# Moving the token counts behind the third unit of the first expert, and h splits and a conversion behind the last gates

## The chip, the core and the metric

The kernel runs on one core of one Trainium2 chip, as one program. The metric is the device time in microseconds (us). TensorE (PE) multiplies matrices, and its weight loads (PEld) overlap them; VectorE (DVE), ScalarE (ACT) and GpSimd (POOL) work element by element; SyncE (SP) issues most of the DMA transfers. Each engine works through its own list of instructions and waits on semaphores for the others.

## The reference

Three stages in a row, all in float32, on 2304 tokens (4 batches of 576) with 512 features.

```
phi(x) = exp(h - max h) / sqrt(m),  h = x @ omega.T - |x|^2/2         # random features, q and k
num = phi(q) @ (phi(k).T @ v);  den = phi(q) @ sum(phi(k)) + 1e-6;  x = num / den

logits = normalized(x) @ normalized(expert_emb).T / tau                # routing over 8 experts
expert_idx = argmax(logits);  gate_w = softmax(logits)[expert_idx]
out[mask] = gate_w * (relu(x[mask] @ w1[e]) @ w2[e])                   # for each expert e that has tokens

silu(x @ w_gate) * (x @ w_val) @ w_out                                 # d_ff = 1536; these weights are doubles
```

## The kernel before

A float32 operand is used as two parts (`hi_lo`): ScalarE casts it to the high part (L92), VectorE subtracts to get the low part (L93). A product is then three TensorE products, high with high, high with low, low with high (`HALVES`). Both parts of an operand have to be there before all three can run, but the first two need the high part of the stationary weights alone.

**The first stage** (L420 to L690) goes over 18 tiles of k and 18 of q, 128 tokens each. It writes x transposed into a large tile (`xp`) and collects logits for the routing, in two groups of nine tiles (`Routing`, two batches each). The second group's routing is not finished when the stage ends. What is left of it is `rest`, a generator: softmax, one-hot choice and gates on VectorE (`softmax`, `gates`), then `counts`. `counts` multiplies the one-hot sums `oc` by a matrix of ones (L327), transposes the gates `gt` (L333) and stores them to memory (L336), and finds for each batch the expert that most of its tokens chose (`dom_i`) and how many tokens chose others (`ext_i`, and their total `tot_i`).

**The second stage** runs one expert for each of the four batches, that batch's dominant one, on all 576 tokens. An expert has four units of `mm1` (each 256 columns of the hidden layer, two blocks of 24 products, L884) and then four of `mm2` (48 products each, L903). Each unit fetches its weights (512 KB, L384) into two raw buffers and splits them into `wp` tiles. ReLU (L890, high part) and its low part (L891) follow each block. A table `todo` (from L1035) says what else is written at the end of which unit: `(0, 1): routing_end` means at batch 0, after the second unit. `routing_end` runs `rest` to its end and lets the engines load `tot_i` into a register (L1008), by which they branch past a loop for tokens of other experts. In that loop nothing runs where the total is zero. The weight splits of the third unit are held in program order.

**The third stage** computes both gated products (12 slices of the hidden layer, named f, by three groups of tokens, named g) with seven products instead of eight (L1120), in the PSUM tiles `a`, `b` and `c`. `tokens` writes after each product what ScalarE, VectorE and GpSimd do with it: copies, sums (L1085), silu (L1088), and the last product (L1091, L1092), which goes to memory as `hds` (L1093). Beside it the doubles are turned into float32 by integer work (`words`: one step on ScalarE, L782, five on VectorE, L784 to L802).

**The fourth stage** is the output product (L1191). For f from 0 to 11 it loads h (`hidden`, 128 by 1024, L1183), splits it, and adds three products for each of eight token tiles into eight PSUM tiles `o_ps`, which take the banks that the third stage held. Output weights `wos` are converted two at a time, by `out_ahead`, and split by `out_weights`.

The order of each engine's list is made by a scheduler with a model of the engines' times; only some instructions are held in the order in which the program is written (`keep_in_program_order`), or behind one that is named (`issue_after`). In the stretch of the counts, ScalarE's copy L335, its load L1008 and the third unit's weight cast L92 follow one another.

Of the kernel before, what the change touches and what calls it, by code (L numbers as in the profile page):

```python
# [14 lines left out]
AF = mybir.ActivationFunctionType  # L15
ALU = mybir.AluOpType
# [12 lines left out]
def attention_moe_ffn_kernel(  # L29
# [815 lines left out]
    with ExitStack() as p2:  # L845
# [184 lines left out]
        def split_begin():  # L1030
# [2 lines left out]
            tc.keep_in_program_order(nc.scalar.activation(out=silu_set, in_=zero, func=AF.Silu))  # L1033

        todo = {  # L1035
            (0, 1): routing_end, (0, NU - 1): no_y,
            (0, NU + NC - 2): near_extras, (0, NU + NC - 1): extras,
            (2, 0): lambda: weights_ahead(0), (2, NU - 1): lambda: list(split_y(0)),
            (3, 0): lambda: weights_ahead(1), (3, NU - 1): lambda: list(split_y(1)),
# [27 lines left out]
    with ExitStack() as p3:  # L1067
# [7 lines left out]
        def tokens(f, g):  # L1075
# [9 lines left out]
                nc.vector.tensor_tensor(out=out, in0=bank_of[k], in1=out, op=ALU.add)  # L1085

            def silu(x):
                nc.scalar.activation(out=x, in_=x, func=AF.Silu)  # L1088

            def last_product():  # L1090
                nc.vector.tensor_tensor(out=cc[:, 0], in0=bank_of["a"], in1=cc[:, 0], op=ALU.mult)  # L1091
                nc.gpsimd.tensor_tensor(out=cc[:, 1], in0=c22, in1=cc[:, 1], op=ALU.mult)  # L1092
                nc.sync.dma_start(  # L1093
                    out=hds[f][:, g * GW:(g + 1) * GW], in_=cc.rearrange("p a n -> p (a n)")
                )
# [80 lines left out]
    with ExitStack() as p4:  # L1176
        op = p4.enter_context(tc.tile_pool(name="op", bufs=6, reuse_waits="tile"))
        ops = p4.enter_context(tc.tile_pool(name="ops", bufs=8, space=PSUM, reuse_waits="tile"))

        def hidden(f, t0, n, slot, width):  # L1180
            raw = wpool.tile([128, 2, NC * FU], F32, tag="wp", name="h32")
            raw = raw.rearrange("p a n -> p (a n)")[:, 0:n * 128]
            nc.sync.dma_start(out=raw, in_=hds[f][:, t0 * 128:(t0 + n) * 128])  # L1183
            at = slot * 2 * width
            h = arena[:, at:at + 2 * n * 128].rearrange("p (a n) -> p a n", a=2)
            hi_lo(h[:, 0], h[:, 1], raw)
            return h

        def product(p, h, f, i):
            for k, (x, a) in enumerate(HALVES):  # L1190
                nc.tensor.matmul(  # L1191
                    p, h[:, x, i * 128:(i + 1) * 128], wos[f][:, a],
                    start=(f == 0 and k == 0), stop=(f == NF - 1 and k == 2),
                )

        def store(p, t):
            o = op.tile([128, DM], F32, tag="o", name="o")
            nc.scalar.copy(o, p)  # L1198
            nc.sync.dma_start(out=out[t * 128:(t + 1) * 128, :], in_=o)

        n_h = 0
        for t0 in range(0, NTI, 8):
            n = min(8, NTI - t0)
            ps = [ops.tile([128, DM], F32, tag="o", name="o_ps") for _ in range(n)]
            if n == 8:
                for f in range(NF):
                    if t0 == 0:
                        if f not in wos:
                            out_weights(f)
                        if f == 1:  # L1210
                            out_ahead(6)
                        elif f in (4, 6):
                            out_ahead(f + 4)
                    h = hidden(f, t0, n, n_h % 3, 1024)
                    n_h += 1
                    for i in range(n):
                        product(ps[i], h, f, i)
                        if f == NF - 1:
                            store(ps[i], t0 + i)
            else:  # L1220
                hs = [hidden(f, t0, n, f, 256) for f in range(NF)]
                for i in range(n):
                    for f in range(NF):
                        product(ps[i], hs[f], f, i)
                    store(ps[i], t0 + i)
# [67 lines left out]
```

## Time and profile before

| | us |
|---|---|
| median of 3 runs | 789.08 (787.39 to 791.02) |
| the profiled execution | 789.36 |
| its span, first to last instruction | 787.3 |
| TensorE matmuls busy | 762.6 (97%) |
| VectorE busy | 506.3 (64%) |
| ScalarE busy | 361.8 (46%) |
| GpSimd busy | 153.4 (19%) |
| mean granted clock of TensorE | 0.988 |

The span is the time that the profile shows; the execution's own time lies 2.1 us above it. TensorE is nearly always busy, so a busy share of another engine says little: what counts is which instruction TensorE waits for. [...]

### The profile page before, as it was taken

To read this page: it belongs to the slowest core of one execution; us is meant where nothing else is said; L and a number is where in the kernel's file an instruction comes from. 1 tells how busy PE (TensorE), PEld (TensorE's weight loads), DVE (VectorE), ACT (ScalarE), POOL (GpSimd) and SP (SyncE) were. 2 spreads that over 40 slices of the span, in tenths; PEclk is the share of its full clock that TensorE was granted. 3 is DMA by queue.
4 is the path that set the end of the run, shared out by engine and by line. 5 is a ranking of instruction groups with operands and counts; after the bars stand their busy time and mean duration, and the time that the engine had idled before them with its cause. 6 is when DMAs were issued, how large, how long until landed. Compare 5 with 4: busy or idle time off the path is not lost.

```text
span 787.3 us, 14727 instructions
## 1 busy us (share of the span) xinstructions
PE 762.6 (97%) x5860; PEld 713.7 (91%) x5861; DVE 506.3 (64%) x878; ACT 361.8 (46%) x789; POOL 153.4 (19%) x201
## 2 busy tenths in 40 slices
PE   9999899959999999999999999999999999999997
PEld 8877777859999999999999999999999988888886
DVE  5788999554243478585887776898887777212220
ACT  5888668553132243343554444444454633241231
POOL 3864344200001404104111111111211110000000
PEclk9999989979999999999999999999999999999999
DMA  8744642122233323420132232233323555353233
GB/s 276 218 143 160 201 147 99 42 83 83 82 98 134 96 82 134 97 107 1 41 114 94 94 134 94 95 134 124 122 111 112 172 169 158 113 210 107 81 98 116
DMA packets 33908, 94.02 MB, mean 119 GB/s; under 512 B 4240, under 2 KB 8352, under 8 KB 33832
## 3 DMA queue, kind: packets, MB, share of 16 engines
q1 hardware_dynamic: 33672, 92.99, 35.3%
q8 instruction: 47, 0.77, 0.4%
q14 instruction: 29, 0.24, 0.1%
q10 hardware_dynamic: 160, 0.02, 0.0%
HBM read 74.05 MB, written 18.95 MB: 118 GB/s over the span
## 4 chain that ended last, share of the span: by engine, by line
PE 70%; DVE 1%; DMA 1%; issue 1%; ACT 0%; ACTq 0%; DVEq 0%
PE o_ps L1191 19%; PE a L1120 18%; PE b L1120 9%; PE two L884 7%; PE two L903 5%; PE third L903 5%; PE c L1120 5%; PE third L884 2%; DMA h<-hds 1%; DVE xp L93 0%; DVE cc L1085 0%; DVE cv_t L798 0%; ACT xp L92 0%; DVE raw L795 0%; ACT o L1198 0%
## 5 line engine op out<-in xcount | busy, mean ns | idle before, releaser
L1191 PE MATMUL o_ps<-xp 128*128 128x512 f32 x648 | 147.5, 389 | 0.7 <-DVE cc L1091 0.4
L1191 PEld LDWEIGHTS o_ps<-xp 128*128 128x128 f32 x648 | 121.5, 188 | 26.6 <-DVE cc L1091 0.8
L504 ACT ACTIVATE ph<-two,bias 128x128 f32<-128x128 f32 x288 | 78.1, 387 | 29.4 <-DVE bias L495 23.1
L93 DVE TENSOR_TENSOR xp<-h,xp 128x1024 fp32r<-128x1024 f32 (+1 forms) x36 | 34.4, 958 | 82.3 <-ACT xp L92 81.8
L884 PE MATMUL two<-xp,wp 128*128 128x288 f32 x576 | 82.0, 301 | 4.5 <-ACT wp L92 2.5
L884 PEld LDWEIGHTS two<-xp,wp 128*128 128x128 f32 x576 | 79.5, 193 | 5.3 <-ACT wp L92 2.8
L1092 POOL TENSOR_TENSOR cc<-c,cc 128x384 f32<-128x384 f32 x36 | 39.8, 1110 | 225.0 <-ACT cc L1088 191.9
L930 POOL TENSOR_TENSOR y_g<-y_g,t 128x192 f32<-128x192 f32 (+3 forms) x29 | 37.3, 1306 | 181.5 <-DVE t L915 181.5
L92 ACT CAST xp<-h 128x1024 fp32r<-128x1024 f32 (+1 forms) x36 | 30.0, 838 | 79.1 <-PE o_ps L1191 62.0
L92 ACT CAST wp<-raw 128x1024 fp32r<-128x1024 f32 x32 | 33.6, 1049 | 58.4 <-PE two L903 29.5
L1088 ACT ACTIVATE cc<-cc 128x384 f32<-128x384 f32 x72 | 37.3, 525 | 49.7 <-DVE cc L1085 49.5
L903 PE MATMUL third<-h_all,wp 128*128 128x288 f32 x384 | 52.8, 296 | 0.0
L903 PE MATMUL two<-h_all,wp 128*128 128x288 f32 x384 | 52.2, 296 | 0.0
L903 PEld LDWEIGHTS third<-h_all,wp 128*128 128x128 f32 x384 | 51.7, 189 | 0.0
L903 PEld LDWEIGHTS two<-h_all,wp 128*128 128x128 f32 x384 | 51.5, 189 | 0.0
L487 DVE TENSOR_REDUCE mx<-two 128x8 f32<-128x1024 f32 x36 | 43.9, 1220 | 8.3 <-PE two L477 8.1
L93 DVE TENSOR_TENSOR wp<-raw,wp 128x1024 fp32r<-128x1024 f32 x30 | 39.9, 1329 | 11.0 <-ACT wp L92 10.7
L1120 PE MATMUL a<-xp,over_y 128*128 128x384 f32 x216 | 43.3, 335 | 0.0
L1120 PEld LDWEIGHTS a<-xp,over_y 128*128 128x128 f32 x216 | 38.3, 188 | 0.0
L1120 PE MATMUL a<-xp,wh 128*128 128x384 f32 x144 | 37.0, 338 | 0.0
L891 DVE SCALAR_TENSOR_TENSOR h_all<-two,h_all 128x576 fp32r<-128x576 f32 x24 | 18.1, 756 | 26.2 <-ACT h_all L890 26.2
L890 ACT ACTIVATE h_all<-two 128x576 fp32r<-128x576 f32 x24 | 15.5, 652 | 38.7 <-PE two L884 38.7
(211 smaller groups left out, 1529.5 us busy)
## 6 DMA issues: line engine op xcount, KB each, us to landing
raw<-in_w_dram SPq DMA_DIRECT2D x68, 512.0 KB, 3.7
hds<-cc SPq DMA_DIRECT2D x36, 384.0 KB, 2.3
h<-hds SPq DMA_DIRECT2D x24, 512.0 KB, 3.5
q<-in_qx_dram SPq DMA_DIRECT2D x18, 512.0 KB, 3.6
k<-in_kx_dram SPq DMA_DIRECT2D x14, 512.0 KB, 4.5
v<-in_vx_dram SPq DMA_DIRECT2D x18, 276.0 KB, 4.2
out_dram<-o SPq DMA_DIRECT2D x18, 256.0 KB, 2.6
h<-hds SPq DMA_DIRECT2D x12, 128.0 KB, 2.2
```

What stands on the lines that cost most here:

```text
L92: go = nc.scalar.copy(hi, src)
L93: low = lo_eng.tensor_tensor(out=lo, in0=src, in1=hi.bitcast(F32), op=ALU.subtract)
L487: nc.vector.tensor_reduce(out=mx.rearrange("p (c a) -> p a c", a=2), in_=p.rearrange("p a (h m) -> p a h m", m=M), axis=AX.X, op=ALU.max,)
L504: nc.scalar.activation(out=ph[:, h, :], in_=p[:, h % 2, h // 2 * M:(h // 2 + 1) * M], func=AF.Exp, bias=bias[:, h:h + 1],)
L884: nc.tensor.matmul(ps[:, j], w[:, a, c, f * 128:(f + 1) * 128], xv[:, c, b, j * HB:(j + 1) * HB], start=(c == 0 and n == 0), stop=(c == NC ...
L891: nc.vector.scalar_tensor_tensor(out=h2[:, 1], in0=ps, scalar=0.0, in1=h2[:, 0].bitcast(F32), op0=ALU.max, op1=ALU.subtract,)
L903: late["mark"][ENG.PE] = nc.tensor.matmul(ps[:, j], w[:, a, f, :], h[:, b, j * HB:(j + 1) * HB], start=(f == 0 and n == 0), stop=(f == len ...
L930: nc.gpsimd.tensor_tensor(out=yv, in0=yv, in1=t, op=ALU.add)
L1088: nc.scalar.activation(out=x, in_=x, func=AF.Silu)
L1092: nc.gpsimd.tensor_tensor(out=cc[:, 1], in0=c22, in1=cc[:, 1], op=ALU.mult)
L1120: nc.tensor.matmul(bank_of[k], wq_at(f, wq, a)[:, c * 128:(c + 1) * 128], factor(g, xq, x)[:, c], start=(k not in begun), stop=(n == 5), s ...
L1191: nc.tensor.matmul(p, h[:, x, i * 128:(i + 1) * 128], wos[f][:, a], start=(f == 0 and k == 0), stop=(f == NF - 1 and k == 2),)
```

## The change

Three things are done. The end of the routing moves from behind the second unit of the first expert to behind the third. The split of the second and the third h (f = 1 and 2 of the first eight token tiles) is queued behind the last silu and the last gated product. The conversion of the doubles for f = 6 and 7 that is started beside f = 1 is queued there too. Behind the gated product the line numbers of the new kernel are higher by 2 to 14.

```diff
         todo = {
-            (0, 1): routing_end, (0, NU - 1): no_y,
+            (0, 2): routing_end, (0, NU - 1): no_y,
...
             def silu(x):
-                nc.scalar.activation(out=x, in_=x, func=AF.Silu)
+                late["mark"]["silu"] = nc.scalar.activation(out=x, in_=x, func=AF.Silu)
 
             def last_product():
-                nc.vector.tensor_tensor(out=cc[:, 0], in0=bank_of["a"], in1=cc[:, 0], op=ALU.mult)
+                late["mark"]["gated"] = nc.vector.tensor_tensor(
+                    out=cc[:, 0], in0=bank_of["a"], in1=cc[:, 0], op=ALU.mult
+                )
...
+        def behind_gates():
+
+            stack = ExitStack()
+            for name in ("silu", "gated"):
+                stack.enter_context(tc.issue_after(late["mark"][name].ins))
+            return stack
+
         def hidden(f, t0, n, slot, width):
...
-            hi_lo(h[:, 0], h[:, 1], raw)
+            if t0 == 0 and f in (1, 2):
+                with behind_gates():
+                    hi_lo(h[:, 0], h[:, 1], raw)
+            else:
+                hi_lo(h[:, 0], h[:, 1], raw)
             return h
...
                         if f == 1:
-                            out_ahead(6)
+                            with behind_gates():
+                                out_ahead(6)
```

The order changes on ScalarE where the counts were. The third unit's weights are `wp_2900` before and `wp_2844` now; `wp_2959` belongs to the fourth unit, `wp_3088` and `wp_3033` to the second matrix. Before:

```order
L92 CAST wp_2959<-raw_2957 128x1024
L890 ACTIVATE h_all_2715<-third_2788 128x576
L890 ACTIVATE h_all_2715<-two_2815 128x576
L289 ACTIVATE lg_2842<-lg_2842 128x72
L335 COPY gt_t_2873<-one_2871 72x128
L1008 TENSOR_LOAD tot_i_95
L92 CAST wp_2900<-raw_2898 128x1024
L92 CAST wp_3088<-raw_3086 128x1024
```

And now, in the same place on ScalarE:

```order
L92 CAST wp_2959<-raw_2957 128x1024
L890 ACTIVATE h_all_2715<-third_2788 128x576
L890 ACTIVATE h_all_2715<-two_2815 128x576
L92 CAST wp_2844<-raw_2842 128x1024
L289 ACTIVATE lg_2901<-lg_2901 128x72
L92 CAST wp_3088<-raw_3086 128x1024
L890 ACTIVATE h_all_2715<-two_2847 128x576
L890 ACTIVATE h_all_2715<-third_2874 128x576
L92 CAST wp_3033<-raw_3031 128x1024
L335 COPY gt_t_2932<-one_2930 72x128
```

The third unit's cast stands three places further ahead, behind the second ReLU of the second unit. The load of `tot_i` is gone from this stretch; it stands now ahead of the branch.

TensorE's list behind the last transposes of logits (L269), before:

```order
L269 MATMUL one_2705<-ident_74,lt_2684 128x16 x3
L327 MATMUL one_2867<-oc_2856,ones_72 128x16
L333 MATMUL one_2871<-ident_74,gt_2865 72x128
L884 MATMUL two_2903<-xp_97,wp_2900 128x288 x4
L884 MATMUL third_2930<-xp_97,wp_2900 128x288 x4
```

And now:

```order
L269 MATMUL one_2705<-ident_74,lt_2684 128x16 x3
L884 MATMUL two_2847<-xp_97,wp_2844 128x288 x4
L884 MATMUL third_2874<-xp_97,wp_2844 128x288 x4
L884 MATMUL two_2962<-xp_97,wp_2959 128x288 x18
L884 MATMUL two_2847<-xp_97,wp_2844 128x288 x20
L884 MATMUL third_2874<-xp_97,wp_2844 128x288 x20
L327 MATMUL one_2926<-oc_2915,ones_72 128x16
L333 MATMUL one_2930<-ident_74,gt_2924 72x128
```

The two products of the counts stand 66 products of the third and fourth unit further back. On SP, the store of the gates (L336) likewise moves behind two weight loads.

VectorE's list where the third stage ends; `h32_9212` and `h32_9244` are the second and third h, `cc`, `c22`, `a` and `b` belong to the last two groups of tokens, and `9203` and `9204` to the conversion. Before:

```order
L787 TENSOR_SCALAR cv_t_9204<-cv_t_9204 128x1024
L791 SCALAR_TENSOR_TENSOR w32_9203<-raw64_9200,cv_t_9204 128x1024
L93 TENSOR_TENSOR xp_97<-h32_9212,xp_97 128x1024
L1085 TENSOR_TENSOR c22_9039<-a_9036,c22_9039 128x384
L795 TENSOR_SCALAR raw64_9200<-w32_9203 128x1024
L1085 TENSOR_TENSOR c22_9051<-a_9048,c22_9051 128x384
L93 TENSOR_TENSOR xp_97<-h32_9244,xp_97 128x1024
L1085 TENSOR_TENSOR cc_9040<-b_9037,cc_9040 128x384
L798 SCALAR_TENSOR_TENSOR cv_t_9204<-raw64_9200 128x1024
L1085 TENSOR_TENSOR cc_9052<-b_9049,cc_9052 128x384
L1091 TENSOR_TENSOR cc_9040<-a_9036,cc_9040 128x384
L1091 TENSOR_TENSOR cc_9052<-a_9048,cc_9052 128x384
```

And now:

```order
L93 TENSOR_TENSOR xp_97<-h32_9172,xp_97 128x1024
L1085 TENSOR_TENSOR c22_9039<-a_9036,c22_9039 128x384
L1085 TENSOR_TENSOR c22_9051<-a_9048,c22_9051 128x384
L1085 TENSOR_TENSOR cc_9040<-b_9037,cc_9040 128x384
L1085 TENSOR_TENSOR cc_9052<-b_9049,cc_9052 128x384
L1091 TENSOR_TENSOR cc_9040<-a_9036,cc_9040 128x384
L1091 TENSOR_TENSOR cc_9052<-a_9048,cc_9052 128x384
L784 TENSOR_SCALAR cv_t_9204<-cv_t_9204 128x1024
L93 TENSOR_TENSOR xp_97<-h32_9212,xp_97 128x1024
L787 TENSOR_SCALAR cv_t_9204<-cv_t_9204 128x1024
L93 TENSOR_TENSOR xp_97<-h32_9244,xp_97 128x1024
L791 SCALAR_TENSOR_TENSOR w32_9203<-raw64_9200,cv_t_9204 128x1024
```

The six gate operations stand together, ahead of the second and third h and of the whole conversion. ScalarE's list changes in the same way: its two last silus come before the conversion's first step and the casts of these h. On SP, the store of the last two gated groups moves ahead of the load of the fourth h.

## Rows read from the trace of the kernel before

**Rows 1.** The page, busy time of each engine, share of the span, instructions.
```profile
PE 762.6 (97%) x5860; PEld 713.7 (91%) x5861; DVE 506.3 (64%) x878; ACT 361.8 (46%) x789; POOL 153.4 (19%) x201
```

**Rows 2.** Waits of TensorE: us in total, times, longest us.
```profile
PE one L327 <- DVE oc L302: 4.0, 1, 4.0
PE two L884 <- ACT wp L92: 2.5, 1, 2.5
```

**Rows 3.** Timeline of TensorE, 163 to 189: start, us, what [idle before <-releaser].
```profile
163.41 0.35 PE L269 MATMUL one<-ident,lt 16*128 16x16 f32 x3
167.79 0.37 PE L327 MATMUL one<-oc,ones 128*128 128x16 f32 x2 [4.03 <-DVE oc L302]
170.11 0.40 PE L333 MATMUL one<-ident,gt 128*72 128x128 f32 x1 [1.95 <-DVE cand L161]
173.01 1.33 PE L884 MATMUL two<-xp,wp 128*128 128x288 f32 x4 [2.51 <-ACT wp L92]
...
188.26 0.96 PE L903 MATMUL third<-h_all,wp 128*128 128x288 f32 x6
```

**Rows 4.** Timeline of ScalarE, same stretch.
```profile
166.09 0.65 ACT L890 ACTIVATE h_all<-two 128x576 fp32r<-128x576 f32 x1
166.62 0.27 ACT L289 ACTIVATE lg<-lg 128x72 f32<-128x72 f32 x1
...
171.92 1.04 ACT L92 CAST wp<-raw 128x1024 fp32r<-128x1024 f32 x1 [1.11 <-DVE tot_i L353]
```

**Rows 5.** Chain that ended last: start, us, what.
```profile
226.09 6.40 PE two L884 x48
...
375.51 1.05 PE a L1120 x6
```

**Rows 6.** Half-microsecond stretches: TensorE busy (instructions), granted clock, DMA share, GB/s.
```profile
110.00:110.50 0.50, 0.50 (x4) 0.62 0.37 148
...
113.50:114.00 0.50, 0.50 (x17) 0.97 0.49 147
...
168.00:168.50 0.50, 0.16 (x2) 0.65 0.52 66
...
178.00:178.50 0.50, 0.50 (x4) 0.61 0.00 0
```

**Rows 7.** Timeline of VectorE at the branch.
```profile
214.12 0.76 DVE L915 TENSOR_TENSOR t<-third,gate 128x576 f32<-128x576 f32 x1 [4.15 <-PEq L995]
```

**Rows 8.** Timeline of TensorE where the third stage ends.
```profile
632.76 1.34 PE L1120 MATMUL a<-over_y 128*128 128x384 f32 x6
...
635.43 1.66 PE L1191 MATMUL o_ps<-xp 128*128 128x512 f32 x6 [0.28 <-DVE cc L1085]
637.49 2.81 PE L1191 MATMUL o_ps<-xp 128*128 128x512 f32 x11 [0.40 <-DVE cc L1091]
```

**Rows 9.** The page's groups: busy us, mean ns | idle before.
```profile
L1191 PE MATMUL o_ps<-xp 128*128 128x512 f32 x648 | 147.5, 389 | 0.7 <-DVE cc L1091 0.4
```

**Rows 10.** Timeline of VectorE, 631 to 652.
```profile
633.69 1.22 DVE L93 TENSOR_TENSOR xp<-h,xp 128x1024 fp32r<-128x1024 f32 x1
...
635.29 1.22 DVE L798 SCALAR_TENSOR_TENSOR cv_t<-raw 128x1024 f32<-128x1024 uint32 x1
...
645.64 0.69 DVE L784 TENSOR_SCALAR cv_t<-cv_t 128x1024 f32<-128x1024 f32 x1 [3.96 <-ACT cv_t L782]
...
650.10 1.23 DVE L798 SCALAR_TENSOR_TENSOR cv_t<-raw 128x1024 f32<-128x1024 uint32 x1
```

**Rows 11.** Timeline of SP (issues) and ScalarE, 636 to 660.
```profile
636.53 0.81 SPq L766 DMA_DIRECT2D raw<-in_w_dram  x2
644.49 1.12 ACT L782 ACTIVATE cv_t<-raw 128x1024 f32<-128x1024 f32 x1 [3.61 <-DMA raw<-in_w_dram]
...
651.35 0.81 SPq L766 DMA_DIRECT2D raw<-in_w_dram  x2
657.25 1.12 ACT L782 ACTIVATE cv_t<-raw 128x1024 f32<-128x1024 f32 x1 [3.49 <-DMA raw<-in_w_dram]
```

## The prediction

> **What bounds the kernel now.** I read the page's busy shares first: TensorE's matmuls cover 762.6 of 787.3 us [rows 1], so the only time to be had is where TensorE itself stands still or runs at its lower clock; a faster VectorE or ScalarE is worth nothing by itself. Then the waits of TensorE, longest first: the top ones, 4.0 and 2.5 us, lie in one place, where the first expert meets the end of the routing [rows 2]. The timeline of TensorE shows that place whole: the last transposes of logits start at 163.41, and the stream of expert products starts again only at 173.01 [rows 3]. Between them stand just the two products of the token counts (L327, for the ones-matrix sum, and L333, the transpose of the gates), each waiting for VectorE. [...] Last, the timeline where the gated products end and the output product begins, since the rest of the diff is there: two short holes, before 635.43 and before 637.49, both released by VectorE [rows 8]. Elsewhere the chain of waits runs on TensorE almost without a break.
>
> **Part one: the counts move behind the third unit.** In the order of before, ScalarE does a cast and two ReLUs of the second unit, then the exponential, then the copy of the gates (which waits for L333), then the load of the total from memory, and only then the cast of the third unit's weights. That cast starts at 171.92, and the stream follows it at 173.01 [rows 3, 4]. In the new order the cast stands directly behind the second ReLU, in the exponential's place at 166.62 [rows 4]. Its weights are no new wait: ScalarE was held there by the total, not by a transfer. So the cast moves from 171.92 to 166.62, and TensorE starts again 5.30 us earlier, at 167.71.
>
> What that does to the clock: of the stretch from 173.01 to the first product of the second matrix at 188.26, the 96 products took 15.25 us; at full clock 48 take 6.40 [rows 5], so 96 take 12.80. The loss, 2.45 us, fell in the 5.4 us from 173.01 to 178.4: 0.45 us lost for each microsecond at the lower level. The hole does not vanish: TensorE still stands from 163.76 to 167.71, so I expect the clock to fall at 168.15 as before. How long will it stay down? The nearest row is the spell from 110.1 to 113.5: it lasted 3.4 us, and TensorE was busy in all of it [rows 6]. The long spell of 10.2 us held 5 us in which TensorE had next to nothing to do. With the stream running from 167.71, I take 3.4 us: 1.54 us lost in place of 2.45, a gain of 0.91. Bounds: no fall at all gains the 2.45; 10.2 us again, now all inside the stream, loses 4.6, that is 2.15 worse than before.
>
> [...]
>
> What the moved pieces cost: the two count products stood in the hole for nothing and now stand inside the stream, 0.37 and 0.40 us [rows 3], so up to 0.77 us lost; I take all of it (the lower end is 0, since small products elsewhere overlap). Their inputs, one-hot sums and gates, are by then some microseconds old. The copies on VectorE and ScalarE that follow are small and TensorE needs none of them for the second matrix. On SP, the store of the gates moves behind two weight loads; this frees them, since a load of weights no longer queues behind L333. Its reader is the third batch's gate row, far later. The load of the total now stands on VectorE just ahead of the branch. There VectorE waits 4.15 us for TensorE anyway [rows 7]; in before, ScalarE took less than 1.11 us for it with the wait included [rows 4], so it is hidden, and would cost under 1 us uncovered. The first expert index is read by SP after it is written in both orders. Part one: 5.30 + 0.91 - 0.77 = 5.44 us.
>
> **Part two: splits and conversion behind the last gates.** The last two sets of six gated products start at 632.76; six take 1.05 us [rows 5], so they should end at 634.86, and the output product's first six, at 147.5 / 648 = 0.228 us each [rows 9], at 636.23. The seventh came at 637.49 [rows 8]. The hole is 1.26 us in all. Its cause is on VectorE: the split of an h from 633.69 (1.22 us) and a step of the conversion from 635.29 (1.22) stand ahead of the sums and products that free the PSUM banks [rows 10]. In the new order, all six gate operations come first. Each can follow its own products within about half a microsecond, and the eight output banks are free when TensorE comes to them. I take 1.26 us; the lower bound of the gain is what the delayed splits take back.
>
> These splits have room: TensorE needs the second h one f later, 24 x 0.228 = 5.5 us behind 634.86, at 640.3, and the third at 645.8. VectorE is through with the gates at about 635.5; a step of conversion (0.69) and the split (1.22) [rows 10] put the second h at 637.5, the third, another such pair, at 639.4. So margins of 2.8 and 6.4 us: cost nothing. What gets later is the chain of doubles. The buffer is free, and the next load issued, when L798 has read it: in before from L784 at 645.64 to L798's end at 651.33, 5.7 us with one split between [rows 10]; with two splits 6.9, so at 642.5 in place of 636.53. A load took 636.53 to 644.49 or 651.35 to 657.25, 8.0 or 5.9 us, and from its landing to the next issue 6.9 [rows 11]. ScalarE has the second conversion's first step ahead of the eighth h, and VectorE its reading steps too. Two loads, one interval and 8.1 us (interval and split) give 642.5 + 11.8 + 15.0 = 669.3 with the short load, 673.5 with the long. TensorE wants the eighth h at 634.86 + 7 x 5.47 = 673.1. So between 3.8 us early and 0.4 late: I take nothing.
>
> **Sum.** 5.44 + 1.26 = 6.70 us. The profiled execution took 789.36 us (span 787.3 and 2.1 around it), 0.28 over the median of 789.08 and inside 787.39 to 791.02. 789.36 - 6.70 = **782.7 us**. Behind the first place nothing but TensorE's own stream sets the time, so what is won there should arrive at the end.
>
> **Rivals.**
> - *The clock does not fall.* The hole shrinks from nine microseconds to four. For it: the fall came at the very end of what is left of the hole, 0.4 us behind the new start. Against: the spell at 110.1 came with TensorE nearly always busy [rows 6]. Gain 5.30 + 2.45 - 0.77 + 1.26 = 8.24: 781.1 us.
> - *The low spell stays as long as it was.* For it: 10.2 us is what this place showed. Against: half of it had no work. Gain 5.30 - 2.15 - 0.77 + 1.26 = 3.64: 785.7 us.
> - *The second part gives nothing*: another VectorE wait takes the holes' place, or the h splits come as late as the banks did. For it: ScalarE and VectorE are fully in order and have as many operations as before. Against: margins of 2.8 us and more. 783.9 us.
> - *Slower.* The chain of doubles holds up the eighth h and what follows it. ScalarE's cast for that h stands behind the conversion's wait for its load, and so do all later casts. It starts to cost once the two loads together pass 15.6 us, and each microsecond more is one of TensorE's; to eat 6.7 us they must take 22.3, over 11 each, against 8.0 at most in the rows [rows 11]. At 12 each it is 24 - 15.6 = 8.4 lost and a total of 791.1 us. [...]
>
> **Chances.** Forecast 0.63, no fall 0.12, long spell 0.10, second part nothing 0.12, slower 0.03. A measurement of this kernel can tell about 0.5%, 3.9 us, from no change: faster than 785.1 is the forecast, no fall, second part nothing, and little of the long spell; its rest, and a part of the forecast's spread, lie within the 0.5%. Faster 0.86, same 0.11, slower 0.03. The range runs from 780.6, no fall with half a microsecond of scatter, to 785.9, the long spell; the executions of before lie 2 us either side of their median, which is more than the other terms' bounds add.
>
> **What would show it.** Right: the first product behind the last logits at about 167.7; the count products behind the third unit's second block, with no idle time before them; a low clock of 3 to 4 us; the second matrix's first product 5 to 6 us earlier than 188.26; no VectorE wait ahead of the output product; no idle on TensorE in the output stage. Wrong: a wait of the third unit on its weights or banks, a low clock beyond 174, idle time ahead of the eighth h, or a gain at 188 that is gone when the next expert begins.

## The result, and the profile after

The changed kernel took **780.87 us** (median of six executions, 778.28 to 782.11) beside 789.35 us for the kernel before (six, 787.39 to 791.02): a ratio of 0.9891, with a 95% interval of 0.9871 to 0.9911. That is 8.5 us gained; 6.7 were forecast, and 780.87 lies inside the range, close to its lower end. The profiled execution of the changed kernel took 780.39 us, with a span of 778.4.

The page of the changed kernel: first its busy line, then the group of the output product, whose line number is 1204 now (busy us, mean ns, idle before).

```profile
PE 760.4 (98%) x5860; PEld 712.6 (92%) x5861; DVE 506.2 (65%) x878; ACT 361.7 (46%) x789; POOL 153.0 (20%) x201
...
L1204 PE MATMUL o_ps<-xp 128*128 128x512 f32 x648 | 147.1, 389 | 0.0
```

TensorE's busy time is nearly what it was, 760.4 us for 762.6 [rows 1]; most of what went is idle time, 24.7 us before (787.3 - 762.6) and 18.0 now (778.4 - 760.4). The output product has no idle time in front of it any more, where [rows 9] showed 0.7 us. Of the two waits at the top of [rows 2], one is left:

```profile
PE two L884 <- ACT wp L92: 4.0, 1, 4.0
```

The timeline of TensorE at that place, to be laid beside [rows 3]:

```profile
163.34 0.35 PE L269 MATMUL one<-ident,lt 16*128 16x16 f32 x3
167.66 1.05 PE L884 MATMUL two<-xp,wp 128*128 128x288 f32 x4 [3.97 <-ACT wp L92]
...
178.13 0.29 PE L327 MATMUL one<-oc,ones 128*128 128x16 f32 x2
178.27 0.28 PE L333 MATMUL one<-ident,gt 128*72 128x128 f32 x1
178.31 4.24 PE L884 MATMUL two<-xp,wp 128*128 128x288 f32 x30
182.39 3.90 PE L903 MATMUL third<-h_all,wp 128*128 128x288 f32 x28
```

The stream starts again at 167.66, the two count products (L327, L333) stand inside it with no wait of their own, and the second matrix begins at 182.39. From the last transposes of logits to there it took 24.85 us before and takes 19.05 now. The reason stands on ScalarE, where the cast now stands ahead of the exponential (compare [rows 4]):

```profile
166.55 1.05 ACT L92 CAST wp<-raw 128x1024 fp32r<-128x1024 f32 x1
167.49 0.28 ACT L289 ACTIVATE lg<-lg 128x72 f32<-128x72 f32 x1
```

The clock, in half microseconds (busy time of TensorE with instructions, granted clock, DMA share, GB/s), still falls, from 1.00 to 0.50, but comes back at 171.4 (0.57 is 0.43 us at 0.50 and the rest at 1.00); [rows 6] had it down until 178.4:

```profile
168.00:168.50 0.50, 0.50 (x4) 0.51 0.46 74
168.50:169.00 0.50, 0.50 (x3) 0.50 0.42 123
...
171.00:171.50 0.50, 0.50 (x5) 0.57 1.05 197
171.50:172.00 0.50, 0.50 (x5) 1.00 0.71 147
```

One more difference had not been in my sum. Behind the branch (releaser L995 on TensorE's sequencer), the kernel before stopped after nine products for 1.54 us, in which it waited for nothing that the profile shows ("issue"). Its timeline there:

```profile
214.47 1.42 PE L884 MATMUL two<-xp,wp 128*128 128x288 f32 x9 [0.45 <-PEq L995]
217.43 4.79 PE L884 MATMUL two<-xp,wp 128*128 128x288 f32 x34 [1.54 <-issue]
```

In the changed kernel, the 48 products run in one piece:

```profile
208.60 6.87 PE L884 MATMUL two<-xp,wp 128*128 128x288 f32 x48 [0.45 <-PEq L995]
```

Where the gated products end, TensorE passes to the output product without a stop (compare [rows 8]):

```profile
626.32 1.20 PE L1122 MATMUL a<-h_all,over_y 128*128 128x384 f32 x6
627.36 12.90 PE L1204 MATMUL o_ps<-xp 128*128 128x512 f32 x56
```

VectorE does each gate half a microsecond behind its products, and the conversion's steps and the splits follow (the first one shown; compare [rows 10]):

```profile
626.52 0.56 DVE L1091 TENSOR_TENSOR cc<-a,cc 128x384 f32<-128x384 f32 x1 [0.48 <-PE a L1122]
627.56 0.56 DVE L1091 TENSOR_TENSOR cc<-a,cc 128x384 f32<-128x384 f32 x1 [0.48 <-PE a L1122]
628.03 0.68 DVE L784 TENSOR_SCALAR cv_t<-cv_t 128x1024 f32<-128x1024 f32 x1
```

**Where the 8.9 us between the two spans went.** Each number is a difference of starts in the two profiled executions:

| stretch | before | after | gain, us |
|---|---|---|---|
| up to the last transposes of logits | 163.41 | 163.34 | 0.07 |
| from there to the second matrix | 24.85 | 19.05 | 5.80 |
| from there to the branch | 26.21 | 26.21 | 0.00 |
| from the branch to the first gated product | 155.51 | 153.94 | 1.57 |
| from there to the first output product | 265.45 | 264.82 | 0.63 |
| the stop before the seventh output product: 637.49 - 635.43 - 6 x 0.228 | 0.69 | 0 | 0.69 |
| sum | | | 8.76 |

The rest, 0.14 us, is scattered.

### The profile page after: what moved, and what is told of

Its sections match the earlier page's. It is cut to its first block, busy times and chain, and to the rows that moved or that the text cites. A ratio compares the mean times of both kernels' runs of the same rounds, so it can differ in the third digit from the quotient of the medians.

```text
span 778.4 us, 14727 instructions
## 1 busy us (share of the span) xinstructions
PE 760.4 (98%) x5860; PEld 712.6 (92%) x5861; DVE 506.2 (65%) x878; ACT 361.7 (46%) x789; POOL 153.0 (20%) x201
## 4 chain that ended last, share of the span: by engine, by line
PE 73%; ACT 0%; issue 0%; ACTq 0%
PE a L1122 19%; PE o_ps L1204 19%; PE b L1122 10%; PE two L884 7%; PE two L903 5%; PE third L903 5%; PE c L1122 5%; PE third L884 2%; ACT o L1211 0%; ACTq L1211 0%
## 5 line engine op out<-in xcount | busy, mean ns | idle before, releaser
L890 ACT ACTIVATE h_all<-two 128x576 fp32r<-128x576 f32 x24 | 15.6, 654 | 35.5 <-PE two L884 35.5
```

## The experiments

In the table, "restart" is the time from the last transposes of logits to the second matrix; "branch" is the time from the branch to the first gated product. The kernel before, run beside them on the same chip, had medians of 789.36, 789.34 and 789.88 us for the runs 1 to 4, 5 to 8 and 9 to 12. Ahead of what was changed the profiled executions differ by some 2 us (the last transposes of logits start at 163.00 in run 3 and at 165.26 in run 2), so single times are good to that, and stretches of one trace to better. The two stretches come from one profiled execution of each kernel.

| run | us, median (executions) | ratio, 95% interval | restart | branch |
|---|---|---|---|---|
| before | 789.35 (6) | | 24.85 | 155.51 |
| changed | 780.87 (6) | 0.9891 [0.9871, 0.9911] | 19.05 | 153.94 |
| 1, part one alone | 782.77 (6) | 0.9912 [0.9894, 0.9929] | 19.64 | 153.68 |
| 2, part two alone | 788.35 (12) | 0.9979 [0.9965, 0.9993] | 24.89 | 155.54 |
| 3, cast first | 783.71 (6) | 0.9922 [0.9905, 0.9939] | 19.09 | 153.68 |
| 4, no hole | 775.87 (5) | 0.9823 [0.9805, 0.9841] | 11.49 | 153.72 |
| 5, six products more | 785.86 (6) | 0.9949 [0.9935, 0.9963] | 24.90 | 150.10 |
| 6, one warm-up product | 783.12 (1) | | 18.89 | 150.09 |
| 7, conversion put back | 780.52 (1) | | 19.15 | 153.70 |
| 8, splits put back | 782.06 (1) | | 19.53 | 153.88 |
| 9, one product more | 791.97 (1) | | 24.99 | 155.39 |
| 10, three products more | 787.92 (1) | | 24.93 | 153.72 |
| 11, twelve products more | 789.90 (1) | | 24.90 | 153.72 |
| 12, no hole, six products more | 776.80 (5) | 0.9843 [0.9829, 0.9856] | 12.77 | 153.70 |

**1. Part one alone.** The kernel before with one edit:

```diff
-            (0, 1): routing_end, (0, NU - 1): no_y,
+            (0, 2): routing_end, (0, NU - 1): no_y,
```

Expected:

> The kernel before with part one alone: the counts behind the third unit. Theory (the third unit's weight cast is what ended last there): TensorE starts again at 167.7, the low clock lasts 3.4 us, the second matrix starts at 182.4, and the two holes ahead of the output product (0.44 and 0.69 us) are as before; total 5.9 us faster. The trace of the changed kernel also lacks a stop of 1.54 us behind the branch (TensorE with nothing it waits for). Rival A: that stop goes because of part one, so 7.4 us faster in every run. Rival B: the stop comes and goes by itself, so 5.9, with or without it in the profile.

It took 782.77 us, 6.6 less than before: between the 5.9 of the theory and the 7.4 of rival A. The restart came as in the changed kernel, but at a low clock that began earlier and lasted twice as long, from 165.8 to 172.65. The timeline of TensorE, and the clock at both ends of the low spell:

```profile
167.78 1.33 PE L884 MATMUL two<-xp,wp 128*128 128x288 f32 x4 [3.97 <-ACT wp L92]
...
183.10 1.09 PE L903 MATMUL third<-h_all,wp 128*128 128x288 f32 x7
```

```profile
165.50:166.00 0.50, 0.00 (x0) 0.82 0.00 0
...
172.50:173.00 0.50, 0.50 (x5) 0.85 0.92 377
```

Of these 6.8 us, two lay in the hole itself; the stretch to the second matrix is only 0.59 us longer than in the changed kernel (19.64 for 19.05). The stop behind the branch is gone here too, which gives 1.83 us (153.68 for 155.51), and both waits of the output product on VectorE are still there (0.4 and 0.3 us). So part one brings the early restart, and part two is not needed for the end of the stop. Most of what is missing from rival A's 7.4 us is the longer low spell.

**2. Part two alone.** The changed kernel with the counts put back:

```diff
-            (0, 2): routing_end, (0, NU - 1): no_y,
+            (0, 1): routing_end, (0, NU - 1): no_y,
```

Expected:

> The changed kernel with the counts put back behind the second unit: part two alone. Theory (splits and conversion steps stood ahead of the gate operations): the holes ahead of the output product are gone, the hole of 9.2 us at 163.8 is there; 1.3 us faster. Rival A (the stop behind the branch goes with part two): 2.8 us faster. Rival B (part two only moves a wait into the output stage): 0 us.

It took 788.35 us, 1.0 us less than before for the 1.3 expected, ratio 0.9979 [0.9965, 0.9993]. The hole is what it was, with the stop behind the branch, so rival A falls; the output product waits for nothing on VectorE and follows 2.08 us behind the start of the last twelve gated products (2.67 in before):

```profile
174.87 1.33 PE L884 MATMUL two<-xp,wp 128*128 128x288 f32 x4 [2.51 <-ACT wp L92]
...
219.37 5.46 PE L884 MATMUL two<-xp,wp 128*128 128x288 f32 x39 [1.59 <-issue]
...
636.72 8.59 PE L1204 MATMUL o_ps<-xp 128*128 128x512 f32 x37
```

The two ratios, 0.9912 [0.9894, 0.9929] and 0.9979 [0.9965, 0.9993], multiply to 0.9891, which is that of the whole change, 0.9891 [0.9871, 0.9911]: within these intervals, the parts add.

**3. The cast first, the counts where they were.** The kernel before, with the third unit's weights fetched ahead of the routing's end and nothing else moved by hand:

```diff
-            (0, 1): routing_end, (0, NU - 1): no_y,
+            (0, 1): lambda: (xs[0].fetch(), routing_end()), (0, NU - 1): no_y,
```

Expected:

> The kernel before with the third unit's weights fetched and cast ahead of the counts, the counts still written behind the second unit; the load of the total stands later too, since the scheduler puts the counts' later parts behind. In the order TensorE has the ones-matrix product still first behind the logits, the transpose of the gates 30 products later. Theory (the cast decides, not where the counts are written): the first count product at 167.7, the stream at 168.0, second matrix at 182.4 to 182.8, 5.5 to 5.9 us faster, as part one. Rival (the counts' products must leave the hole): the stream starts after the one-hot sums and what follows them, 169 or later, and the gain is 4.5 us or less.

It took 783.71 us, and the second matrix began at 182.09:

```profile
167.39 0.36 PE L327 MATMUL one<-oc,ones 128*128 128x16 f32 x2 [4.03 <-DVE oc L302]
...
173.18 0.27 PE L333 MATMUL one<-ident,gt 128*72 128x128 f32 x1
...
182.09 1.09 PE L903 MATMUL third<-h_all,wp 128*128 128x288 f32 x7
```

L327 stands at the end of the same hole, and the stream follows it at 167.60; L333 found its place in the stream. The restart is worth 19.09 us, as in the changed kernel (19.05). So what the restart hangs on is the cast's place ahead of the load of the total on ScalarE, not on L327 leaving the hole. L333 did leave it in this run, so its place is not tested apart. The stop behind the branch is gone here as well. Its end and the early restart together would be worth more than the 5.65 us gained; 1.2 us of it are lost again in the gated products up to their last twelve, 0.49 us of that in a stop at their beginning on ScalarE's result, which before does not have.

**4. What is left of the hole.** In the changed kernel the cast at 166.55 still stood behind the writing of zeros to y on ScalarE and behind the cast at 164.53. The zeros are twelve copies (changed kernel):

```profile
157.21 7.43 ACT L1016 COPY y_g<-zero 128x192 f32<-128x192 f32 x12
```

Here, GpSimd writes the zeros, and the third unit's load is issued a unit earlier (the two edits were not run apart):

```diff
-                    nc.scalar.copy(y, zero.to_broadcast([128, y.shape[1]]))
+                    nc.gpsimd.memset(y, 0.0)
...
-            (0, 2): routing_end, (0, NU - 1): no_y,
+            (0, 0): lambda: xs[0].fetch(), (0, 2): routing_end, (0, NU - 1): no_y,
```

Expected:

> The changed kernel with two more edits: the twelve fills of y with zeros go from ScalarE (7.4 us, 157.2 to 164.6) to GpSimd, and the third unit's weights are fetched behind the first unit, so that their cast stands ahead of the second unit's ReLUs. Theory (the rest of the hole is ScalarE's fills in front of that cast, and the low clock comes from the hole): TensorE goes on behind the logits without a stop, no clock fall between 160 and 185; 4.0 + 1.5 = 5.5 us faster than the changed kernel, 13 to 14 faster than before. Rival A (the clock falls at about 168 whatever TensorE does): 4.0 us faster than the changed kernel. Rival B (VectorE, which has the routing to do, becomes the wait: low parts and banks come late): under 3 us faster than the changed kernel, with VectorE as releaser.

It took **775.87 us**, 5.0 less than the changed kernel, 13.5 less than before and the best of all, near what the theory said; rival A, with a clock that falls whatever TensorE does, is out. TensorE has no idle time there, and the clock reads 1.00 in the half microseconds from 166.0, 168.0 and 171.0 (the middle one shown):

```profile
165.14 0.35 PE L269 MATMUL one<-ident,lt 16*128 16x16 f32 x3
165.42 1.45 PE L884 MATMUL two<-xp,wp 128*128 128x288 f32 x9
...
176.63 5.63 PE L903 MATMUL third<-h_all,wp 128*128 128x288 f32 x41
```

```profile
168.00:168.50 0.50, 0.50 (x6) 1.00 0.00 0
```

More products of the first units now stand ahead of the logits, so the second matrix's start is what compares: 176.63 for 182.39, 5.76 us earlier. A stop of 0.50 us at the first gates on ScalarE's result, which the changed kernel does not have, takes a part back.

**5. The stop behind the branch, moved by instructions alone.** The kernel before, with six products of the ones matrix in TensorE's idle time, ahead of the transpose of the gates. They do no needed work, and nothing else changes its order:

```diff
+            [nc.tensor.matmul(p[:, 0:E], ones, ones[:, 0:E], start=True, stop=True) for _ in range(6 if g else 0)]
             nc.tensor.transpose(p[:PT * E, :], self.gt.rearrange("p i e -> p (i e)"), ident)
```

Expected:

> The kernel before with six more products of the ones matrix with itself (8 columns) on TensorE just ahead of the transpose of the gates (L333), where TensorE stands idle for 1.95 us; nothing else moves on any engine. Theory: the stop of 1.54 us behind the branch, nine products in, comes from where TensorE's pieces of program happen to end; six more products, some 1.5 KB of instructions, put the piece's end earlier, its load (queue q8 instruction) falls ahead of the branch, the 48 products behind the branch run in one piece of 6.5 to 6.9 us, and the time is 1.5 us shorter, ratio 0.998. Rival: the stop belongs to where the counts, the load of the total and the weights' loads stand in time; these have not moved, so it stays at 1.5 us and the ratio is 1.000. Second rival: the load moves, but the stop with it to another place.

It took 785.86 us, ratio 0.9949 [0.9935, 0.9963]. The restart is 24.90 us as before, so the six cost nothing; behind the branch the stop is gone, and the stretch up to the gated products is 5.4 us shorter, not 1.5:

```profile
216.32 6.49 PE L884 MATMUL two<-xp,wp 128*128 128x288 f32 x48 [0.45 <-PEq L995]
...
275.69 6.40 PE L884 MATMUL two<-xp,wp 128*128 128x288 f32 x48
281.93 3.28 PE L884 MATMUL third<-xp,wp 128*128 128x288 f32 x24
```

So the stop goes without any move of the counts. But the load did not fall ahead of the branch, as the theory had it: it was issued 0.1 us behind (in before, 0.7 behind). In the profiled executions 1.8 of the 5.4 us are lost again at the start, where the last transposes of logits come at 165.22 for 163.41. The other 3.9 us come from a quicker pace over some 1,150 products: from 275.69 to 281.93, 48 products took 6.24 us, 130.0 ns each. The same stretch of the kernel before:

```profile
277.13 6.56 PE L884 MATMUL two<-xp,wp 128*128 128x288 f32 x48
283.53 3.36 PE L884 MATMUL third<-xp,wp 128*128 128x288 f32 x24
```

Here they took 6.40 us, 133.3 ns each, with a granted clock of 1.00 in both stretches.

**6. One warm-up product in place of eight**, in the changed kernel, so that TensorE's program is shorter ahead of the branch:

```diff
-            for _ in range(8):
+            for _ in range(1):
                 nc.tensor.matmul(p[:, 0, 0:128], ones, ones, start=True, stop=True)
```

Expected:

> The changed kernel with one warm-up product of the ones matrix at the start of TensorE's program in place of eight; the scheduler then also exchanges a few products far from the branch. Theory of the program pieces: seven products fewer, some 1.8 KB of instructions, make the load 1.9 us later against the products; in the changed kernel it fell 1.1 to 1.6 us ahead of the first product behind the branch, so it would fall just behind it, and a stop of 1 to 1.6 us comes back some ten products in. Rival (the stop belongs to the old place of the counts): 48 products in one piece as in the changed kernel, 6.6 to 6.9 us. The clock and the start of the program may also differ by a few us, which says nothing here.

No stop came back: the 48 products took 6.49 us in one piece, and the load stayed 1.3 us ahead of the branch, where seven products fewer should have put it just behind. The expectation fell. The quick pace is here as well, 150.09 us. The total, 783.12 us, says little, since the first 26 us of the program became 6 us longer.

**7 and 8. Splits and conversion apart.** Both are the changed kernel with one thing put back, the counts staying where they were moved. In the seventh, the conversion of doubles went back to its old place; in the eighth, the splits:

```diff
-                            with behind_gates():
-                                out_ahead(6)
+                            out_ahead(6)
```

```diff
-            if t0 == 0 and f in (1, 2):
+            if t0 == 0 and f in ():
```

Expected of the seventh, and of the eighth:

> The changed kernel with the conversion of doubles in its old place; the counts and the two splits stay moved. The steps of the conversion (0.69 to 1.89 us each on VectorE) again stand between the last sums and products of the gates, and one step more than before. Theory: the holes ahead of the output product are VectorE's queue, so about 1.3 us of the waits of o_ps on VectorE come back (0.7 to 1.6), span 779.5. Rival: the splits alone were the cause, no wait of o_ps over 0.2 us.

> The changed kernel with the two splits in their old place; the counts and the conversion stay moved. One split (1.22 us) stands between the sums as before, the conversion's steps do not. Theory: most of the hole ahead of the output product is gone, 0.0 to 0.5 us of waits of o_ps on VectorE left. Rival: split and conversion had each an equal share, so about 0.6 us is left.

Seventh: 780.52 us and no wait of the output product. My expectation fell, its rival stood. VectorE's timeline shows why: the conversion's steps do stand between the gates, but the gates are done in time all the same, the last at about 629, and TensorE, which begins the output product at 627.39, goes on without a stop.

```profile
625.99 1.01 DVE L1085 TENSOR_TENSOR cc<-b,cc 128x384 f32<-128x384 f32 x2
626.92 1.21 DVE L802 TENSOR_TENSOR w<-w,cv_t 128x1024 f32<-128x1024 f32 x1
628.05 1.01 DVE L1091 TENSOR_TENSOR cc<-a,cc 128x384 f32<-128x384 f32 x2
```

```profile
627.39 12.89 PE L1204 MATMUL o_ps<-xp 128*128 128x512 f32 x56
```

Eighth: 782.06 us, and one wait of the output product is left, where before had two:

```profile
627.28 1.20 PE L1122 MATMUL a<-h_all,over_y 128*128 128x384 f32 x6
628.81 11.40 PE L1204 MATMUL o_ps<-xp 128*128 128x512 f32 x49 [0.33 <-DVE cc L1085]
```

The place itself separates them. From the start of the last twelve gated products to the first output product it is 2.67 us in before (632.76 to 635.43), 2.08 in the changed kernel (625.28 to 627.36), 2.08 in the seventh (625.31 to 627.39) and 2.71 in the eighth (626.10 to 628.81); the second stop, 0.69 us, is in before alone. So before lost 1.28 us there, the eighth 0.63 and the seventh nothing. By these single traces the splits make the first hole, and the second needs the conversion beside them. The longer stretch, from the first gated product on, is no measure of this, since it can hold other losses (1.2 us up to the last twelve in run 3).

**9 to 11. The stop, step by step.** The fifth experiment again, with one, three and twelve products in place of six. Expected:

> The kernel before with one more product of the ones matrix ahead of L333 in TensorE's idle time. Theory (the stop behind the branch comes where a piece of TensorE's program ends): one product, two passes, puts the end of the piece two passes earlier, so the stop of 1.5 us comes after seven products behind the branch, where before had nine; the 48 products behind it keep their 6.40 us. Rival (the stop belongs to a moment, not to an instruction): after nine again, or none at all as with six more products.

> The kernel before with three more products of the ones matrix ahead of L333. Theory of the program pieces: the stop comes after three products behind the branch, six earlier than in before. Rival (a moment): after nine. If the stop is gone with three as it was with six, then what makes it is only told to lie between. On the pace behind the branch (133.3 ns for one product of 288 columns in before, 130.0 with six more): if the pace goes with the instructions' place, three may have either; it is 153.7 us from the branch to the gated products at the slow pace and 150.1 at the quick one, both without the stop.

> The kernel before with twelve more products of the ones matrix ahead of L333; they take 4.9 us at the low clock where 1.95 are idle, so the hole grows by up to 3 us. Theory of the program pieces: the piece's end now lies well ahead of the branch, so no stop behind it, as with six. The pace behind the branch, 133.3 or 130.0 ns, tells whether the quick one belongs to six products alone. Rival (a moment): the stop is back, since the branch comes later again.

With one product (two passes), the stop came after seven products, where it had come after nine:

```profile
216.71 1.16 PE L884 MATMUL two<-xp,wp 128*128 128x288 f32 x7 [0.45 <-PEq L995]
219.42 4.81 PE L884 MATMUL two<-xp,wp 128*128 128x288 f32 x35 [1.56 <-issue]
```

This is what the theory of the program's pieces said, to the product: in this one trace the stop moved with the instructions and did not keep its moment behind the branch. With three products it should have come after three, and was gone:

```profile
214.51 6.63 PE L884 MATMUL two<-xp,wp 128*128 128x288 f32 x48 [0.45 <-PEq L995]
```

With twelve it was gone too, though the load was issued 0.6 us behind the branch and not well ahead of it. So the theory was borne out with one product and failed with three and in run 6; with six and twelve the stop went, but not in the way that the theory gives.

In the run with twelve the hole did not grow, either. The scheduler had put the cast ahead of the gates' copy (L335, at 175.29), and the cast still waited for the total:

```profile
173.68 1.04 ACT L92 CAST wp<-raw 128x1024 fp32r<-128x1024 f32 x1 [4.97 <-DVE tot_i L353]
```

L333 came 2.9 us later behind the logits than in before, and the restart is the same, 24.90 us: it is the total, and not the transpose of the gates, that holds the cast. The pace was the slow one in all three (133.3 ns; 153.72 us without a stop), so six products had hit something that one, three and twelve do not.

**12. Both together.** The fourth kernel with the six products of the fifth, which stand inside its stream. Expected:

> The fourth experiment (zeros of y on GpSimd, third unit's load earlier, the changed kernel otherwise) with six more products of the ones matrix ahead of L333, which now stand inside the stream. If the quick pace behind the branch comes with these six as it did in the kernel before, the stretch from the branch to the gated products takes 150.1 us in place of 153.7, the six cost 0.7 to 1.3 us at the full clock, and the time is 773.3 us (772.8 to 773.8), 2.6 us under the fourth experiment. If the pace hangs on the place of each instruction in the program, which is another one here, it stays at 133.3 ns and the time is 776.8.

It took 776.80 us, 0.9 more than the fourth: the six products lengthen the restart by 1.28 us (12.77 for 11.49), and the pace stayed at 133.3 ns (153.70 us). So the six products that came with the quick pace in run 5 did not bring it here. That it hangs on where the instructions come to lie was the expectation's other branch; it is not shown.

## Why the prediction came out as it did

**The restart, right.** Forecast: 5.30 us earlier. Measured against the last transposes of logits, the stream started again 9.60 us behind them before (173.01 - 163.41) and 4.32 now (167.66 - 163.34): 5.28. The wait of 3.97 us that is left on the cast is the hole that the forecast left standing. The third experiment shows that it is the cast's place on ScalarE that does it, and run 11 that the total was what held it.

**The clock, right in kind, a little off in size.** It fell near the forecast moment (168.0 for 168.15) and stayed down 3.4 us, as taken. Its two levels are seen in the trace of before, 0.50 behind the fall and 1.00 behind the return, so that the 0.65 and 0.61 of [rows 6] put the fall at 168.15 and the return at 178.4:

```profile
168.50:169.00 0.50, 0.00 (x0) 0.50 0.16 66
...
178.50:179.00 0.50, 0.50 (x6) 1.00 0.07 16
```

From the restart to the second matrix it took 14.73 us; 12.80 of that are the products at the full clock and 0.18 the count products, so 1.75 were lost, not 1.54, and the gain is 2.45 - 1.75 = 0.70, not 0.91. In the changed kernel and in runs 1, 3, 7 and 8, which restart near 167.6, the clock was back between 171.3 and 172.7, not at 178.4. So in these runs an earlier stream came with an earlier end of the spell. Run 11 does not fit so simply: its twelve small products kept TensorE occupied from 169.81 until the stream started at 174.90, and the low spell was still 10.2 us long (169.92 to 180.16), as in before:

```profile
169.50:170.00 0.50, 0.41 (x4) 0.92 0.00 0
...
180.00:180.50 0.50, 0.50 (x5) 0.84 0.00 0
```

So what ends a spell is not shown. The two ends are not fixed, either: in runs 1 and 8 the spell was 6.8 us long, by beginning 2.2 to 2.4 us earlier and ending 1.0 to 1.2 later. Such a spell costs 0.5 to 0.6 us more (19.64 and 19.53 for 19.05), since it begins where TensorE stands idle anyway. That the middle value came in the changed kernel's profile and not 6.8 us is luck, worth that half microsecond. The 10.2 us of the rival came in no run with the early restart.

**The count products, over-priced.** Taken at 0.77 us; the products behind them start 0.18 us late (178.31 for 178.13). Their durations in the timeline are 0.29 and 0.28 us, but these overlap with the neighbours: the starts are 0.14 and 0.04 us apart. Inside this stream, the distance of starts is the price, 0.14 + 0.04 = 0.18 us.

**The holes ahead of the output product, right in sum.** Forecast 1.26 us; measured 0.63 + 0.69 = 1.32. I had put them down to the split and the step of the conversion alike. The seventh and eighth experiments show no need for moving the conversion once the splits are moved: with it in its old place the output product waits for nothing, while the splits alone, in theirs, cost 0.63 us.

**The chain of doubles, right.** The forecast had the load issued at 642.5 by the clock of before; it was issued at 634.74, which is 642.8 when the 8.07 us gained up to there (635.43 for 627.36) are added. The two loads then took 5.5 and 4.9 us, so nothing was late, and the rival that ended on the slower side never came near its 15.6 us. The rows of SP and ScalarE that answer to [rows 11]:

```profile
634.74 0.82 SPq L766 DMA_DIRECT2D raw<-in_w_dram  x2
640.25 1.16 ACT L782 ACTIVATE cv_t<-raw 128x1024 f32<-128x1024 f32 x1 [0.24 <-DMA raw<-in_w_dram]
646.14 0.81 SPq L766 DMA_DIRECT2D raw<-in_w_dram  x2
651.03 1.15 ACT L782 ACTIVATE cv_t<-raw 128x1024 f32<-128x1024 f32 x1 [0.52 <-DMA raw<-in_w_dram]
```

**What was missing.** The weak step is the sentence that, elsewhere, the chain runs on TensorE "almost without a break". The kernel before had a break of 1.54 us right behind the branch, and I priced nothing for it. It stood in the same list of waits as [rows 2]:

```profile
PE two L884 <- issue: 1.5, 1, 1.5
```

(The list has waits of up to 2.0 us in the first stage as well; the change left them.) The end of the stop is 1.57 us of the 8.76. The terms that were priced at 6.70 us came to 7.12 (5.28 + 0.70 - 0.18 + 1.32), so on them the forecast was good to 0.4, most of it the over-priced counts. That the time still lies in the range, 0.3 us from its end, is partly luck: the range was wide for other reasons, and nothing in it allowed for this stop.

Shown are that the stop goes with part one (run 1) or with the cast's move (run 3), that it stays when the order ahead of the branch stays (run 2), that it also goes without any move of the counts (runs 5, 10, 11), and that one small product moved it by the two passes put in (run 9). Not shown is what makes it come or go. The number of products is not it: before, the changed kernel and runs 1 to 3 all have 2548 ahead of the branch. The trace shows single transfers of 0.02 MB on the queue "q8 instruction", in before 47 of them with 0.77 MB together, which I took for the loads of TensorE's program. Shared among its 5860 products and 5861 weight loads that is 66 bytes each, an estimate; by it six products (12 passes with their 12 weight loads) make 1.6 KB and seven 1.8, beside the 1.5 and 1.8 in the expectations of runs 5 and 6. One such transfer came about 0.7 us behind the branch in the two kernels with nine products, and 1.3 us ahead of it in the changed kernel. But with three more products it came 0.5 us behind, with six 0.1 and with twelve 0.6, and there was no stop; with one more it came 0.2 us behind and there was one. So the load's moment alone does not tell it, and that the stop belongs to these loads at all is a guess.

## What to carry to other kernels

In an engine's list, look for what stands behind a wait without needing it: here one cast stood on ScalarE behind a load of a scalar that TensorE did not need yet, until 171.92 [rows 4], and its place alone brought the second matrix 5.8 us forward (run 3), while the products that seemed to be the matter cost 0.18 us inside the stream. The hole that was shortened to 4 us still came with a spell of low clock (3.4 us in the changed kernel, 6.8 in runs 1 and 8); taking it away whole, as the fourth experiment did, brought 5.0 us more. Read the "issue" pieces in the list of waits, above all behind a branch: here one of 1.5 us came and went with small changes of order and number ahead of it, in a way that no run explains. A change can gain or lose that much by no merit of its own, and it is to be subtracted before its reason is judged.

## What the runs showed of the hardware that I had not expected

- A stop of 1.54 to 1.59 us behind a branch (in before and in runs 2 and 9), which came after seven products in place of nine with one dummy product of two passes (run 9), and was not there with three, six or twelve (runs 10, 5, 11).
- Two paces for the same products at the same granted clock, 1.00: 133.3 ns (before) or 130.0 ns (run 5) for one of 288 columns. The quick one came in two kernels (runs 5 and 6), each time only behind the branch (150.1 us to the gated products for 153.7), with six dummy products more or seven warm-up products fewer, and not with one, three or twelve more. Each is known from one trace. What sets it is open.
- With the same 4 us of idle time the low clock began 2.2 to 2.4 us earlier in two kernels (runs 1 and 8) than in the changed one (at 165.8 and 165.6 for 168.0) and lasted 6.8 us in place of 3.4. With twelve small products in the hole of before (run 11) it lasted 10.2 us, as without them. With no idle time at that place (run 4) it read 1.00 at 166.0, 168.0 and 171.0; the mean granted clock of that execution is 0.997.
